# Operands of the output weights made straight from float64 in the expert layer, converted in the tile of their results; token sums moved

## The chip, the cores and the metric

One of the 8 cores of a Trainium2 chip runs the whole program. The metric is the device time of one execution in microseconds (us), as the median of several executions. One execution was also taken by the hardware profiler; it gives the rows below.

## The reference

Three stages follow each other on 2304 tokens of width 512.

```python
# 1: attention inside chunks of 64 tokens, 4 x 8 heads of width 64
scores = scale * np.matmul(q_c, k_c.transpose(0, 1, 2, 4, 3))
attn = np.exp(scores - np.max(scores, axis=-1, keepdims=True))
attn = attn / (np.sum(attn, axis=-1, keepdims=True) + 1e-09)
x = heads_joined(np.matmul(attn, v_c))              # (2304, 512)
# 2: expert layer, 4 experts, hidden width 1024
p = domain_probs / (domain_probs.sum(-1, keepdims=True) + 1e-09)
for e in range(4):
    out += p[:, e:e + 1] * (np.maximum(x @ w1[e], 0.0) @ w2[e])
# 3: gated layer, hidden width 1536, on the result of 2
g = x @ w_gate
y = (g * (1.0 / (1.0 + np.exp(-g))) * (x @ w_val)) @ w_out
```

`w_gate`, `w_val` and `w_out` come as float64 (two words a number), all else as float32.

## The kernel before

**Numbers.** TensorE multiplies in the form float32r. So that nothing is lost, each operand is split into a high part `h`, rounded by ScalarE, and a low part `l`, the rest, subtracted by GpSimd or VectorE (`split`, `w_split`, lines 126 and 127). Each product takes three matmuls: h h, h l, l h.

**Products.** Layers 2 and 3 use Strassen's scheme on 2 x 2 blocks, with 7 products (`PRODUCTS`) in place of 8. Its operands are blocks and sums of blocks: of the weights (`w_sums`, `w_split`) and of the tokens (`b11` to `b22`, `t1` to `t4`). A *set* is the 7 products of 256 hidden columns. The tokens go through in 3 passes of 768. The expert layer has 16 sets a pass (numbers 0 to 47), the gated layer 12 (48 to 83: a set of `w_gate` and one of `w_val` in turn). A product is 6 matmuls of 384 columns into a bank x, z or w (`half_k`, lines 632 to 634). Between products stand the matmuls of the second half of the layer, a *group* (two sets, or four in the gated layer's count) later: `layer2` (512 columns, lines 681 to 685) for the experts, `layer_out` (256 columns, line 747) for `w_out`.

**Order.** The program writes out the order by hand (`order`). `now` counts products. At each product, work planned with `later(d, ...)` for this count is issued, then the weights of the product six further on are loaded (`LEAD`, `prepare`, `load_w`, line 413), then background tasks take steps (`run_tasks`). All these transfers go through the one queue of SyncE (SP), which issues them in the order of the program and stands wherever one has to wait for its buffer or its data. Weight tiles `w` have 12 buffers, tiles of tokens on their way (`xt`) three, tiles for raw weights (`raw1`) two.

**Background tasks.** A task is a generator. `WAIT` lets a product pass, `STEP` asks for one of the steps that a product grants; four tasks may run. They are:
- `x_sums(p)` (line 181 on): loads blocks of pass p's tokens into two `xt` tiles, makes the four sums `t1` to `t4` on GpSimd, stores them. Twice per pass, for two halves.
- `convert`: makes float32 from float64 by bit operations: a raw load of 512 KB into a `raw64` tile, then 4 instructions on VectorE, 3 on ScalarE, 2 on GpSimd (lines 440 to 454), into `dst`.
- `make_set64(q, m)`: two conversions into a `raw1` tile, the sums, 7 splits, 7 stores into `w_d`, for a set of the gated layer.
- `make_wo(c)`: one conversion of a row block of `w_out`, stored as float32 in `wo_d`.
- `make_wo_ops(g, k)`: loads two such blocks back, makes `t1` to `t4` and splits 7 operands (low parts in turn on GpSimd and VectorE), stores them in `wo_ops`, from which `fetch_wo` loads them for each group.

`make_wo` runs in the expert layer, `make_wo_ops` from set 48 on. At the turn from one pass to the next, `x_fetch` loads the 7 operands of the new pass's tokens into `xt` tiles (line 209) and `x_split` splits them, each after the last use of the old one.

**Start.** Attention of the first six blocks of 128 tokens runs alone, with k and v of blocks 2 and 3 in tiles of their own (`att_load`, `att_load_v`), then twelve products without Strassen (`next_plain`).

## Time and profile before

| | |
|---|---|
| median of 3 executions | 1288.68 us (1286.35 to 1290.72) |
| the profiled execution | 1290.5 us, of which the span from first to last instruction is 1288.7 us |
| mean granted clock of TensorE | 0.985 |
| TensorE busy, matmuls / weight loads | 1242.0 us (96%) / 1142.7 us (89%) |
| VectorE, ScalarE, GpSimd busy | 801.1 us (62%), 538.2 us (42%), 583.5 us (45%) |
| moved by DMA | 366.24 MB, 284 GB/s in the mean |

PE is TensorE's matmuls, PEld its weight loads, DVE VectorE, ACT ScalarE, POOL GpSimd, SP the engine that issues nearly all transfers (SPq is its queue). Matmuls overlap, so a busy PE alone does not tell its speed; that is why windows of equal work are compared. A wait is told with what ended it. Names such as `w<-w` are output and input of an instruction by the program's names, buffer numbers left out.

### The profile page before, as it was taken

The numbers are of one execution on the slowest core, as the hardware profiler recorded it, in microseconds if no ns is written. First come the engines' busy times: TensorE is split into PE (matmuls) and PEld (weight loads), VectorE is DVE, ScalarE is ACT, GpSimd is POOL, SyncE is SP. The second block draws the span as 40 slices with busy tenths as digits, with TensorE's granted clock in tenths as the row PEclk, the third lists the DMA queues.
The fourth block names the chain that finished last, engine by engine and source line by source line (L and its number), as shares of the span: only waits on it lengthen the run. The fifth ranks groups of instructions, "written<-read, shape, count | busy, mean of one in ns | idle before, by whom it ended". The sixth has DMA issues, their size and how long they took to land.

```text
span 1288.7 us, 21183 instructions
## 1 busy us (share of the span) xinstructions
PE 1242.0 (96%) x7216; PEld 1142.7 (89%) x7216; DVE 801.1 (62%) x1370; ACT 538.2 (42%) x1192; POOL 583.5 (45%) x593
## 2 busy tenths in 40 slices
PE   7999999998999999999999999999885899999998
PEld 6888888897998999998999888998785899999998
DVE  5775666656655666764665654576573755676566
ACT  4554443445433444443443443455332344344331
POOL 5454343567633555552554654435652522332121
PEclk9999999999999999999999999999896999999999
DMA  8588877789898798888999788788995997698774
GB/s 230 167 280 278 269 261 244 235 296 359 302 320 302 277 335 306 306 296 272 320 318 350 276 303 291 253 288 301 365 344 177 320 347 270 241 318 289 260 248 154
DMA packets 183051, 366.24 MB, mean 284 GB/s; under 512 B 19600, under 2 KB 46736, under 8 KB 182944
## 3 DMA queue, kind: packets, MB, share of 16 engines
q1 hardware_dynamic: 182144, 363.54, 81.1%
q10 hardware_dynamic: 768, 1.31, 0.4%
q8 instruction: 58, 0.95, 0.3%
q14 instruction: 49, 0.40, 0.1%
q0 software_dynamic: 32, 0.04, 0.0%
HBM read 262.05 MB, written 102.76 MB: 283 GB/s over the span
## 4 chain that ended last, share of the span: by engine, by line
PE 81%; DMA 9%; DVE 3%; issue 2%; POOL 2%; SPq 1%; ACT 1%; POOLq 0%; DVEq 0%; ACTq 0%
PE y L681 10%; PE y L685 10%; PE y L683 10%; PE lx L632 7%; PE lx L634 7%; PE lx L633 7%; PE ox L747 4%; PE lz L632 4%; PE lz L634 4%; PE lz L633 4%; PE oz L747 3%; DMA w<-w 3%; PE lw L632 2%; PE lw L634 2%; PE lw L633 2%
## 5 line engine op out<-in xcount | busy, mean ns | idle before, releaser
L681 PE MATMUL y<-w,hh 128*128 128x512 f32 x576 | 228.7, 397 | 2.1 <-ACT hh L567 2.1
L683 PE MATMUL y<-w,hh 128*128 128x512 f32 x576 | 226.3, 393 | 1.7 <-POOL w L127 1.7
L685 PE MATMUL y<-w,hl 128*128 128x512 f32 x576 | 227.1, 394 | 0.0
L127 POOL TENSOR_TENSOR w<-raw,w 128x256 fp32r<-128x256 f32 (+1 forms) x156 | 142.9, 931 | 146.8 <-ACT w L126 121.0
L127 POOL TENSOR_TENSOR ol<-sg,oh 128x384 fp32r<-128x384 f32 x72 | 82.5, 1154 | 230.7 <-ACT oh L126 201.9
L567 ACT ACTIVATE hh<-sum_p 128x384 fp32r<-128x384 f32 x90 | 47.3, 525 | 233.4 <-DVE sum_p L620 233.2
L770 DVE SCALAR_TENSOR_TENSOR acc<-y,prob,acc 128x512 f32<-128x512 f32 x126 | 91.2, 743 | 68.4 <-PE y L685 67.9
L685 PEld LDWEIGHTS y<-w,hl 128*128 128x128 f32 x576 | 108.4, 188 | 24.2
L681 PEld LDWEIGHTS y<-w,hh 128*128 128x128 f32 x576 | 108.5, 188 | 24.0 <-ACT hh L567 2.5
L683 PEld LDWEIGHTS y<-w,hh 128*128 128x128 f32 x576 | 108.5, 188 | 22.8 <-POOL w L127 2.0
L127 POOL TENSOR_TENSOR w_made<-raw,w_made 128x256 fp32r<-128x256 f32 x84 | 67.5, 814 | 103.5 <-ACT w_made L126 94.1
L620 DVE TENSOR_TENSOR sum_p<-lx,p 128x384 f32<-128x384 f32 x81 | 44.9, 555 | 106.3 <-PE lx L634 106.1
L568 DVE SCALAR_TENSOR_TENSOR hl<-sum_p,hh 128x384 fp32r<-128x384 f32 x90 | 58.8, 654 | 61.4 <-ACT hh L567 61.4
L126 ACT ACTIVATE w<-raw 128x256 fp32r<-128x256 f32 (+1 forms) x156 | 67.4, 453 | 3.8 <-POOL w L127 2.5
L453 POOL TENSOR_TENSOR neg<-neg,raw 128x512 f32<-128x512 f32 x24 | 32.3, 1345 | 75.3 <-ACT p L616 32.9
L632 PE MATMUL lz<-t1h,w 128*128 128x384 f32 x162 | 56.3, 348 | 8.3 <-DMA w<-w 8.3
L126 ACT ACTIVATE oh<-sg 128x384 fp32r<-128x384 f32 x72 | 36.5, 524 | 63.6 <-DVE sg L581 63.3
L632 PE MATMUL lx<-t3h,w 128*128 128x384 f32 x162 | 55.5, 342 | 7.8 <-DMA w<-w 7.4
L616 ACT COPY u<-lx 128x384 f32<-128x384 f32 x81 | 38.4, 474 | 58.1 <-PE lx L634 58.1
L632 PE MATMUL lx<-t2h,w 128*128 128x384 f32 x162 | 56.3, 347 | 4.6 <-DMA w<-w 3.3
L632 PE MATMUL lx<-t4h,w 128*128 128x384 f32 x162 | 54.9, 339 | 3.7 <-DMA w<-w 3.7
L632 PE MATMUL lz<-b22h,w 128*128 128x384 f32 x162 | 56.2, 347 | 1.8 <-ACT p L616 1.6
(271 smaller groups left out, 3436.0 us busy)
## 6 DMA issues: line engine op xcount, KB each, us to landing
w<-w SPq DMA_DIRECT2D x567, 256.0 KB, 5.2
w<-w SPq DMA_DIRECT2D x96, 512.0 KB, 5.7
w<-w_made SPq DMA_DIRECT2D x84, 256.0 KB, 5.4
wo_t<-wo_t SPq DMA_DIRECT2D x36, 512.0 KB, 5.2
wo_b<-wo_b SPq DMA_DIRECT2D x27, 512.0 KB, 4.1
raw<-w SPq DMA_DIRECT2D x19, 512.0 KB, 4.3
raw<-w SPq DMA_DIRECT2D x32, 256.0 KB, 4.2
sums<-x SPq DMA_DIRECT2D x40, 192.0 KB, 5.7
```

The lines of the kernel that those rows point to most:

```text
L126: nc.scalar.activation(h, src, AF.Copy)
L127: (lo or nc.vector).tensor_tensor(out=l, in0=src, in1=h.bitcast(F32), op=ALU.subtract)
L567: nc.scalar.activation(h, src, AF.Relu)
L568: nc.vector.scalar_tensor_tensor(out=l, in0=src, scalar=0.0, in1=h.bitcast(F32), op0=ALU.max, op1=ALU.subtract)
L632: nc.tensor.matmul(ps, w[:, 0, c], xh[:, k], start=f, stop=False, skip_group_check=True)
L633: nc.tensor.matmul(ps, w[:, 0, c], xl[:, k], start=False, stop=False, skip_group_check=True)
L634: nc.tensor.matmul(ps, w[:, 1, c], xh[:, k], start=False, stop=e, skip_group_check=True)
L681: nc.tensor.matmul(y, hh[:, c], w[:, 0], start=(j == 0), stop=False)
L683: nc.tensor.matmul(y, hh[:, c], w[:, 1], start=False, stop=False)
L685: nc.tensor.matmul(y, hl[:, c], w[:, 0], start=False, stop=(j == 3))
L747: nc.tensor.matmul(o, left[:, c], w[:, k, right], start=start and t % 2 == 0 and k == 0 and i == 0, stop=k == 1 and i == 2, skip_group_che ...
L770: nc.vector.scalar_tensor_tensor(out=sum_, in0=y, scalar=p, in1=sum_, op0=ALU.mult, op1=ALU.add)
```

## The change

- `make_wo` and `wo_d` are gone. `make_set64` and `make_wo_ops` are now one function, `make_ops`: it loads both raw halves (two times 512 KB) at once into the tile that will hold the results, converts them there, makes the sums, splits 7 operands with all low parts on GpSimd, and stores them. So the operands of `w_out` come from float64 in one go.
- All 18 such tasks run in the expert layer, from set 18 on, a task of `w_out` between the two of a pair of sets. Three may be under way: every third takes the `raw64` tile (one buffer), the others `raw1`. A new kind of step, `SPLIT`, is granted once per product at most. Steps are 2 per product throughout.
- The token sums of pass 2 start with these tasks (two sets later than before), those of pass 4 follow those of pass 3 in the expert layer, those of pass 5 start alone at set 53.
- At the start, v of blocks 2 and 3 comes in two transfers in place of four, `fetch_w1(0)` stands ahead of the first scores, and the first two splits of its weights move ahead by a block.

```diff
@@ -119,7 +119,6 @@
     w2_d = [dram.tile([P, 2, DM], F32, name=f"w2_{c}") for c in range(4 * NG1)]
-    wo_d = [dram.tile([P, DM], F32, name=f"wo_{c}") for c in range(F2 // P)]
     wo_ops = [{b: dram.tile([P, 2, 2, DM // 2], F32, name=f"wo_{b}_{g}") for b in OUT_OPS} for g in range(NG2)]
@@ -196,7 +195,7 @@
                 sub(b[o], b[x], b[y], nc.gpsimd)
-            for _ in range(1 if p > NPASS else 3):
+            for _ in range(3):
                 yield WAIT
@@ -248,6 +247,15 @@
         att[a]["v"] = v
+    def load_values_23():
+        for h in range(2):
+            b = slice(64 * h, 64 * h + 64)
+            nc.sync.dma_start(
+                v23[b, :, h].rearrange("p a i c t -> p a (i c t)"), vt[2:4, b].rearrange("a p i c t -> p a (i c t)")
+            )
+        for i in range(2):
+            att[2 + i]["v"] = vbd[2 + i]
@@ -417,26 +425,22 @@
-    WAIT, STEP = range(2)
-    RAWS, LANDING = 2, 3
-    loads, sets64 = [0], [0]
-    def freed():
-        loads[0] -= 1
-    def convert(dst, src, name):
-        while loads[0] == RAWS:
+    WAIT, STEP, SPLIT = range(3)
+    LANDING = 4
+    sets64, count64, converts = [0], [0], [0]
+    def converted():
+        converts[0] -= 1
+    def convert(raw, dst, name):
+        while converts[0] == 2:
             yield WAIT
-        loads[0] += 1
-        raw = raw64_p.tile([P, 512, 2], U32, tag="raw64", name=f"raw_{name}", bufs=RAWS)
-        nc.sync.dma_start(raw.rearrange("p f w -> p (f w)"), src.bitcast(U32))
-        for _ in range(LANDING):
-            yield WAIT
-        yield STEP
+        converts[0] += 1
         low, up = raw[:, :, 0], raw[:, :, 1].bitcast(F32)
...
         topb, negb = top.bitcast(I32), neg.bitcast(I32)
+        yield STEP
         nc.vector.tensor_scalar(out=top, in0=up, scalar1=F64_MAX, scalar2=-F64_MAX, op0=ALU.min, op1=ALU.max)
@@ -451,52 +455,49 @@
         nc.gpsimd.tensor_tensor(out=neg, in0=neg, in1=low.bitcast(F32), op=ALU.mult)
-        nc.gpsimd.tensor_tensor(out=top if dst is None else dst, in0=top, in1=neg, op=ALU.add)
-        later(2, freed)
-        return top
-    def make_set64(q, m):
-        while sets64[0] == 2:
+        nc.gpsimd.tensor_tensor(out=dst, in0=top, in1=neg, op=ALU.add)
+        later(1, converted)
+    def make_ops(sources, name, sums, stores):
+        while sets64[0] == 3:
             yield WAIT
         sets64[0] += 1
-        r = raw1_p.tile([P, 8, 2 * P], F32, tag="raw1", name=f"raw_{q}_{m}")
+        count64[0] += 1
+        pool, tag = (raw64_p, dict(tag="raw64", bufs=1)) if count64[0] % 3 == 0 else (raw1_p, dict(tag="raw1"))
+        r = pool.tile([P, 8, 2 * P], F32, name=f"raw_{name}", **tag)
+        raws = [r[:, 4 * half : 4 * half + 4].bitcast(U32).rearrange("p b f -> p (b f)") for half in range(2)]
+        for half in range(2):
+            nc.sync.dma_start(raws[half], sources[half].bitcast(U32))
+        for _ in range(LANDING):
+            yield WAIT
         for half in range(2):
             dst = r[:, 2 * half : 2 * half + 2].rearrange("p b f -> p (b f)")
-            yield from convert(dst, (wg, wv)[m][q, half], f"{q}_{m}_{half}")
+            yield from convert(raws[half].rearrange("p (f w) -> p f w", w=2), dst, f"{name}_{half}")
         for half in range(2):
             yield STEP
-            w_sums(r, nc.gpsimd, half)
-        for i in range(NPROD):
-            yield STEP
-            t = w_split(r, PRODUCTS[i][1], f"made_{q}_{m}")
-            later(3, lambda i=i, t=t: nc.sync.dma_start(w_d[NPAIRS + 2 * q + m][i], t.bitcast(F32)))
+            sums(r, half)
+        for a, to in stores:
+            yield SPLIT
+            t = w_split(r, a, f"made_{name}")
+            later(3, lambda to=to, t=t: nc.sync.dma_start(to, t.bitcast(F32)))
         sets64[0] -= 1
-    def make_wo(c):
-        t = yield from convert(None, wo[c], f"wo_{c}")
-        yield WAIT
-        yield WAIT
-        nc.sync.dma_start(wo_d[c], t)
+    def make_set64(q, m):
+        into = w_d[NPAIRS + 2 * q + m]
+        stores = [(PRODUCTS[i][1], into[i]) for i in range(NPROD)]
+        return make_ops((wg, wv)[m][q], f"{q}_{m}", lambda r, half: w_sums(r, nc.gpsimd, half), stores)
     def make_wo_ops(g, k):
-        while sets64[0] == 2:
-            yield WAIT
-        sets64[0] += 1
-        r = raw1_p.tile([P, 8, 2 * P], F32, tag="raw1", name=f"raw_wo_{g}_{k}")
-        for c in range(2):
-            nc.sync.dma_start(r[:, 2 * c : 2 * c + 2].rearrange("p b f -> p (b f)"), wo_d[4 * g + 2 * k + c])
-        for _ in range(LANDING + 1):
-            yield WAIT
         places = {"b11": 0, "b12": 1, "b21": 2, "b22": 3, "t1": 4, "t2": 5, "t3": 6, "t4": 7}
-        for o, x, y in ("t1", "b12", "b11"), ("t2", "b22", "t1"), ("t3", "b22", "b12"), ("t4", "b21", "t2"):
-            yield STEP
-            sub(r[:, places[o]], r[:, places[x]], r[:, places[y]], nc.gpsimd)
-        for i, b in enumerate(OUT_OPS):
-            yield STEP
-            t = w_split(r, places[b], f"wo_{g}_{k}", nc.vector if i % 2 else nc.gpsimd)
-            later(5, lambda b=b, t=t: nc.sync.dma_start(wo_ops[g][b][:, k], t.bitcast(F32)))
-        sets64[0] -= 1
+        ops = ("t1", "b12", "b11"), ("t2", "b22", "t1"), ("t3", "b22", "b12"), ("t4", "b21", "t2")
+        def sums(r, half):
+            for names in ops[2 * half : 2 * half + 2]:
+                o, x, y = (r[:, places[b]] for b in names)
+                sub(o, x, y, nc.gpsimd)
+        c = 4 * g + 2 * k
+        return make_ops(wo[c : c + 2], f"wo_{g}_{k}", sums, [(places[b], wo_ops[g][b][:, k]) for b in OUT_OPS])
@@ -806,9 +807,10 @@
             vbd.append(at_p.tile([P, 2, NPAIR, 2, D], F32, tag=f"v{i}", name=f"vbd{i}", bufs=1))
+        v23 = first_p.tile([P, 2, 2, NPAIR, 2, D], F32, name="v23", bufs=1)
         for i in range(2):
             kbd.append(first_p.tile([P, 2, NPAIR, 2, CH], F32, name=f"kbd{2 + i}", bufs=1))
-            vbd.append(first_p.tile([P, 2, NPAIR, 2, D], F32, name=f"vbd{2 + i}", bufs=1))
+            vbd.append(v23[:, i])
@@ -834,7 +836,8 @@
         att_load(3)
-        att_load_v(2)
+        load_values_23()
+        fetch_w1(0)
@@ -875,8 +878,6 @@
         att_scores(0, where())
-        fetch_w1(0)
-        att_load_v(3)
         att_soft(0)
@@ -889,6 +890,8 @@
                 fetch_w1(1)
+            elif i == 2:
+                w_plain(0, ORDER[:2])
         att_values(2, where())
@@ -896,7 +899,6 @@
         att_exp(4)
-        w_plain(0, ORDER[:2])
         att_scores(5, where())
@@ -966,23 +968,21 @@
-        EARLY = 4
         make64 = []
         for q in range(NPAIRS2):
-            for m in range(2):
-                make64.append(make_set64(q, m))
-                if EARLY <= 2 * q + m + EARLY < 2 * NPAIRS2:
-                    make64.append(make_wo(2 * q + m + EARLY))
+            make64 += [make_set64(q, 0), make_wo_ops(q // 2, q % 2), make_set64(q, 1)]
...
                 running.append([tasks.pop(0), WAIT])
+            splits = 1
             for r in list(running):
-                if r[1] == STEP:
-                    if steps == 0:
+                if r[1] != WAIT:
+                    if steps == 0 or r[1] == SPLIT and splits == 0:
                         continue
                     steps -= 1
+                    splits -= r[1] == SPLIT
                 r[1] = next(r[0], None)
@@ -1071,7 +1071,6 @@
                 wow_p = ctx.enter_context(tc.tile_pool(name="wow", bufs=2, side="right"))
-                tasks += [make_wo_ops(g, k) for g in range(NG2) for k in range(2)]
             product(n, i)
@@ -1106,19 +1105,17 @@
                     tasks.append(x_sums(1))
-            if o == (NPAIRS, 1):
-                tasks += [x_sums(2)] + [make_wo(c) for c in range(EARLY)]
-            elif o == (NPAIRS + 2, 1):
-                tasks += make64
+            if o == (NPAIRS + 2, 1):
+                tasks += [x_sums(2)] + make64
             elif o == (2 * NPAIRS + 3, 1):
-                tasks.insert(0, x_sums(3))
-            elif o == (N1 + 3, 6):
-                tasks.insert(0, (y for p in (4, 5) for y in x_sums(p)))
+                tasks.insert(0, (y for p in (3, 4) for y in x_sums(p)))
+            elif o == (N1 + 5, 4):
+                tasks.append(x_sums(5))
             elif o == (N1 + 3, 2):
...
             if not (last_of_pass(n) or last_of_pass(n + 1) and i >= 5 or now[0] - turned[0] < 2):
-                run_tasks(2 if n < N1 + 4 else 1 + now[0] % 2)
+                run_tasks(2)
             now[0] += 1
```

How SP's queue changes, at three places (`x_70` and `x_69` are token stores of passes 5 and 4, `w_79`, `w_80`, `w_97`, `w_104` the made weights of sets 18, 19, 52, 59, `w_93` those of sets 48, 60 and 72). At the turn from pass 3 to pass 4, before:

```order
L202 DMA xt_75<-sums_4_1_10628 128x384
L192 DMA sums_5_0_10789<-x_70 128x384 x2
L192 DMA sums_5_0_10792<-x_70 128x384 x2
L413 DMA w_2_10805<-w_104 128x512
L512 DMA wo_t_10807<-wo_t_1_162 128x1024
L413 DMA w_3_10842<-w_104 128x512
L209 DMA xraw_b_4_10853<-x_69 128x768
L209 DMA xraw_b_4_10855<-x_69 128x768
L209 DMA xraw_t_4_10857<-xt_75 128x768
L413 DMA w_4_10860<-w_104 128x512
```

and now:

```order
L513 DMA wo_b_10687<-wo_b_1_149 128x1024
L421 DMA w_1_10721<-w_104 128x512
L421 DMA w_6_10740<-w_103 128x512
L421 DMA w_2_10752<-w_104 128x512
L513 DMA wo_t_10754<-wo_t_1_150 128x1024
L421 DMA w_3_10789<-w_104 128x512
L208 DMA xraw_b_4_10800<-x_69 128x768
L208 DMA xraw_b_4_10802<-x_69 128x768
L208 DMA xraw_t_4_10804<-xt_75 128x768
L421 DMA w_4_10807<-w_104 128x512
```

The loads of the sums of pass 5 no longer stand ahead of the fetches of pass 4; before, these sums were stored some 30 rows further down, behind all fetches. Now they are loaded and stored some 20 to 55 rows above the fetches; the last of them:

```order
L513 DMA wo_t_10471<-wo_t_1_146 128x1024
L421 DMA w_3_10506<-w_102 128x512
L421 DMA w_4_10518<-w_102 128x512
L201 DMA xt_76<-sums_5_1_10335 128x384
L201 DMA xt_76<-sums_5_1_10338 128x384
L201 DMA xt_76<-sums_5_1_10335 128x384
L201 DMA xt_76<-sums_5_1_10338 128x384
L421 DMA w_5_10535<-w_102 128x512
```

The last row here follows the last store of the sums; nothing of them is under way at the turn. In the gated layer's first pass (weights of set 52), before:

```order
L413 DMA w_0_9599<-w_97 128x512
L488 DMA raw_wo_0_9607<-wo_141 128x512
L488 DMA raw_wo_0_9607<-wo_142 128x512
L488 DMA raw_wo_1_9610<-wo_143 128x512
L488 DMA raw_wo_1_9610<-wo_144 128x512
L413 DMA w_1_9635<-w_97 128x512
L413 DMA w_6_9646<-w_96 128x512
L512 DMA wo_b_9648<-wo_b_0_149 128x1024
L512 DMA wo_t_9650<-wo_t_0_150 128x1024
L498 DMA wo_b_0_153<-w_wo_0_3_9561 128x512
L498 DMA wo_b_0_153<-w_wo_1_3_9564 128x512
L413 DMA w_2_9664<-w_97 128x512
```

and now:

```order
L421 DMA w_0_9704<-w_97 128x512
L421 DMA w_1_9728<-w_97 128x512
L421 DMA w_6_9739<-w_96 128x512
L513 DMA wo_b_9741<-wo_b_0_137 128x1024
L513 DMA wo_t_9743<-wo_t_0_138 128x1024
L421 DMA w_2_9755<-w_97 128x512
```

The loads and stores that make operands of `w_out` are gone from between the weight loads. In the expert layer, at set 18, before:

```order
L413 DMA w_1_4158<-w_80 128x512
L407 DMA w_79<-w_7_4093 128x512
L432 DMA raw_wo_4175<-wo 128x1024
L520 DMA w_9_1_4186<-w_5_110 128x1024
L413 DMA w_2_4194<-w_80 128x512
```

and now:

```order
L421 DMA w_1_4115<-w_80 128x512
L415 DMA w_79<-w_7_4055 128x512
L191 DMA sums_2_0_4129<-x_67 128x384 x2
L191 DMA sums_2_0_4132<-x_67 128x384 x2
L470 DMA raw_0_4135<-wg 128x1024 x2
L470 DMA raw_wo_0_4138<-wo 128x1024 x2
L470 DMA raw_1_4141<-wv 128x1024 x2
L521 DMA w_9_1_4153<-w_5_110 128x1024
L421 DMA w_2_4161<-w_80 128x512
```

Six raw loads and four loads of tokens now stand in one piece between two weight loads. The order of the matmuls is the same in both kernels.

## Rows read from the trace of the kernel before

**Rows 1.** The page, 40 slices of the span: busy tenths of TensorE's matmuls.
```profile
PE   7999999998999999999999999999885899999998
```
**Rows 2.** Windows (us): length, PE, PEld, DVE, ACT, POOL busy (instructions), clock, DMA share, GB/s.
```profile
864.40:1045.20 180.80, 151.35 (x900) 144.16 (x900) 107.76 (x188) 66.40 (x151) 83.72 (x81) 0.92 0.86 308
1045.20:1179.80 134.60, 133.09 (x883) 131.96 (x883) 89.63 (x176) 56.19 (x121) 39.23 (x33) 1.00 0.79 279
350.20:562.30 212.10, 212.10 (x1067) 191.42 (x1065) 130.79 (x210) 89.91 (x188) 98.38 (x94) 1.00 0.87 306
562.30:797.00 234.70, 234.70 (x1183) 211.52 (x1183) 136.39 (x213) 99.58 (x216) 124.04 (x125) 1.00 0.87 302
676.60:708.80 32.20, 32.20 (x162) 29.00 (x161) 17.56 (x29) 11.90 (x27) 14.34 (x16) 1.00 0.99 350
902.10:934.30 32.20, 26.89 (x150) 25.44 (x150) 18.50 (x32) 12.42 (x32) 20.55 (x22) 0.89 1.00 365
...
966.50:998.70 32.20, 17.50 (x67) 16.44 (x66) 10.00 (x17) 6.54 (x11) 7.61 (x6) 0.69 0.53 178
```
**Rows 3.** Waits of PE, 860 to 1035 us: total us, times, longest us.
```profile
PE lx L632 <- DMA w<-w: 14.5, 4, 7.4
PE lz L632 <- DMA w<-w: 8.3, 6, 3.3
```
**Rows 4.** Timeline of PE: start, duration (us), line, operation, tiles.
```profile
958.52 0.33 PE L632 MATMUL lx<-t3h,w 128*128 128x384 f32 x1
...
985.12 0.52 PE L632 MATMUL lx<-t3h,w 128*128 128x384 f32 x1
```
**Rows 5.** Timeline of SP's queue at the turn from pass 3 to pass 4.
```profile
964.14 0.80 SPq L192 DMA_DIRECT2D sums<-x  x2
...
966.41 8.06 SPq L209 DMA_DIRECT2D xraw_b<-x  x2
980.24 0.32 SPq L209 DMA_DIRECT2D xraw_t<-xt  x1
```
**Rows 6.** Chain of work that ended last, 860 to 1040 us: start, us, what.
```profile
966.41 5.86 DMA xraw_b<-x
```
**Rows 7.** Waits of PE, 1045 to 1180 us.
```profile
PE lz L632 <- DMA w<-w: 0.2, 1, 0.2
```
**Rows 8.** DMA issues: count, KB each, median us from issue to landing.
```profile
w<-w SPq DMA_DIRECT2D x567, 256.0 KB, 5.2
...
sums<-x SPq DMA_DIRECT2D x40, 192.0 KB, 5.7
...
wo_t<-w_wo SPq DMA_DIRECT2D x24, 256.0 KB, 5.2
...
wo_b<-w_wo SPq DMA_DIRECT2D x18, 256.0 KB, 5.8
...
wo<-top_wo SPq DMA_DIRECT2D x12, 256.0 KB, 3.8
raw_wo<-wo SPq DMA_DIRECT2D x12, 256.0 KB, 4.7
```
**Rows 9.** Waits of SP's queue, 350 to 797 us.
```profile
SPq L472 <- POOL w_made L127: 63.2, 36, 6.6
...
SPq L432 <- POOL neg L453: 34.8, 14, 6.0
```
**Rows 10.** Groups on POOL, 350 to 797 us: count, busy us, mean ns, idle before.
```profile
L127 POOL TENSOR_TENSOR w_made<-raw,w_made 128x256 fp32r<-128x256 f32 x83 | 66.7, 814 | 98.7 <-ACT w_made L126 89.3 <-DMA w<-w_made 5.0 <-DMA w<-w 4.3
L397 POOL TENSOR_TENSOR raw<-raw 128x256 f32<-128x256 f32 x48 | 37.8, 809 | 1.8
```
**Rows 11.** One group on DVE, 864 to 1031 us, then 1040 to 1120 us.
```profile
L130 DVE TENSOR_TENSOR sg<-sg,sg 128x384 f32<-128x384 f32 x17 | 15.0, 882 | 5.2 <-POOL ol L127 5.0
...
L130 DVE TENSOR_TENSOR sg<-sg,sg 128x384 f32<-128x384 f32 x12 | 6.7, 556 | 6.1 <-POOL ol L127 5.9
```
**Rows 12.** Timeline of PE in the first slice.
```profile
23.01 1.93 PE L262 MATMUL s<-kbd,q 128*64 128x128 f32 x16 [2.05 <-DMA kbd<-kt]
```

## Prediction before the change was run

> **What bounds the kernel now.** I read the page's slices first, then the windows. TensorE is busy in nearly every slice; the holes are the first slice, one near 300 us, and a group between 870 and 1030 us [rows 1]. The windows say what that group costs [rows 2]. From 350.2 to 797.0 us (weights of the gated layer are made beside the expert layer) PE is busy for all of 212.10 and 234.70 us, although the DMA engines are at 0.87. From 864.4 to 1045.2 us it is busy 151.35 of 180.80 us at a clock of 0.92. The next window, 1045.2 to 1179.8 us, holds the same work one pass later, 84 products and their share of the output layer (set 64 to set 76 instead of 52 to 64), and takes 134.60 us, 133.09 of them busy, at clock 1.00. The counts are close: 900 matmuls against 883, the first having the expert layer's last transposes too. So 180.80 - 134.60 = **46.2 us** are lost in the first pass of the gated layer, and the matmuls' order does not explain it. Of them 29.45 - 1.51 = 27.9 us are idle time and the other 18.3 lie in slower matmuls, 0.65 us for each us of stop.
>
> What PE waits for there: 14.5 us in 4 waits at products into bank x, the longest 7.4, and 8.3 us in 6 at bank z, all for weight loads [rows 3]. Behind the longest, at 985.12 us, a matmul takes 0.52 us that took 0.33 at 958.52 [rows 4]: after such a stop TensorE is at the lower of its two clock levels. Why the weights are late shows on the SP queue [rows 5]. At 964.14 us it issues loads of `sums`, at 966.41 it stands 8.06 us over two loads of `xraw_b`, then nothing before 980.24. The chain of waits gives the first of them 5.86 us [rows 6]; the second is issued some 8 us after the first, once that one is split. The operands of the next pass are fetched one by one because the tag `xt` has three buffers and the token sums of pass 5 hold two across the turn of the pass (first order piece). All weight loads stand behind them. One pass later no sums are under way, and the only wait of PE for a weight load from 1045 to 1180 us is 0.2 us [rows 7].
>
> The smaller part lies before that turn: while the operands of w_out are made, DMA runs full. From 902.1 to 934.3 us share 1.00, 365 GB/s, PE busy 26.89 of 32.20 us [rows 2].
>
> **The change part by part.** The sum is made against the profiled execution: 1290.5 us, of which the span is 1288.7; the median of the runs is 1288.68, so 1.8 us come off at the end.
>
> *Operands of w_out leave the second part.* Out of it go 12 loads of 256 KB (`raw_wo`), 42 stores of 256 KB [rows 8], 42 splits, 24 subtractions; SP issues 24 transfers fewer in all, since the copies in `wo_d` are neither stored nor read. The token sums of pass 4 go with them, and those of pass 5 start at set 53 and are stored before the first fetch of the turn (order pieces). What is left is the work of the twin, so I let the stretch fall to the twin's time: **-46.2 us**.
>
> *Sums of pass 5 stay inside the stretch*, the twin has none: 8 loads and 8 stores of 192 KB [rows 8], 3.1 MB, some 9 us of the queue at 350 GB/s, in a stretch whose DMA share is 0.79. Between 0 (hidden) and 9 us; I take **+1**, since 0.79 leaves room.
>
> *The first part takes over that work.* Removed there: 12 stores of 256 KB (`wo<-top_wo`). Added: 42 stores of 256 KB and the sums of pass 4, 16 transfers of 192 KB [rows 8]; the 12 conversions were there already. Net 42 x 256 - 12 x 256 + 16 x 192 KB, some 11 MB. Over 446.8 us that is 25 GB/s on 304, so share 0.87 becomes about 0.94. The window 676.6 to 708.8 us stood at 0.99 and 350 GB/s with PE busy for all 32.20 us [rows 2]: hidden there. GpSimd gets 42 splits at 814 ns and 24 subtractions at 809 ns [rows 10], 53.6 us on its 98.38 + 124.04 us: from 50% to 62%, off the path as far as no product waits for it (the rival below).
>
> Here a rule speaks against the change. The page DMA: Bandwidth & Descriptors of the Trainium skill (Specifications) gives a core some 358 GB/s of HBM bandwidth. By it, as an estimate, windows that run at 350 GB/s now and are asked for 375 would last 1.05 times as long; if a third of the first part were so, that is 7 us, and the sum below would end at 1253.5. The trace does not hold the chip to that figure, since the window at 902.1 us moved 365 GB/s.
>
> VectorE loses 18 of the 42 low parts to GpSimd, and the two slow each other: the subtraction `sg` took 882 ns from 864 to 1031 us and 556 from 1040 to 1120 [rows 11], where GpSimd is busy 46% and 29% of the stretch [rows 2]. VectorE is busy 267 of 446.8 us in the first part; made longer by 882/556 in the 12% more of the time that GpSimd is busy, 19 us more, 60 to 64%. PE waits for nothing there now, so I cost it at nothing; without that cover it is at most these 19 us.
>
> *Where a set starts.* The raw 512 KB loads now land in the tile of the results, two at once, one product after the last split that read the tile; before it was two products after a conversion. The SP queue already stood for such loads, 34.8 us in 14 times, longest 6.0, and for stores of made weights, 63.2 us in 36 [rows 9], with no wait on PE. Products take 446.8/198 = 2.26 us, weights are loaded six ahead, 13.5 us, and land after 5.2 [rows 8]: 8.3 us in hand. A mean stop of 2.5 us, one product more (2.3) and 0.5 MB more ahead (1.4) leave 2.1; the longest stop (6.0) ends 1.4 us too late. Of 18 starts, with the first three and two token tiles in one product (third order piece), I expect a few late by one or two us, some at the low clock: **+4**. The ends: 0 (the window at 0.99 without a wait) and the rate of 902.1 to 934.3 us (5.3 us idle in 32.2) over all 446.8 us, 74 us. The first is far nearer: same kinds of work, same queue.
>
> *The start.* The first weights and v of blocks 2 and 3 are fetched ahead of k of blocks 4 and 5, with two loads fewer. PE waits 2.05 us for k at 23.01 us [rows 12]; the load can be earlier by its place or later by the 512 KB ahead of it. Between -2 and +2; **-1**. The hole at 318 us has its cause in slow loads and splits at the turn of a pass, before the point where tasks now begin; it stays.
>
> Sum: 1290.5 - 46.2 + 1 + 4 - 1 = 1248.3 for the profiled kind of run, less 1.8: **1246.5 us**.
>
> **The rivals.**
> *The queue becomes the bound of the first part.* For it: 0.94 on average means stretches at 1.00, and at 902.1 us such a stretch cost PE 5.3 us in 32.2. Against: 676.6 to 708.8 us, and at most one split per product now. If a third of the 446.8 us ran at that rate, 24.5 us: 1271; a milder half of that 1259. The rule on 358 GB/s, above, would be its mildest form.
> *The turn still costs.* If the turn from pass 3 to 4 is slow for another reason (fetch and split of seven operands), what is lost from 966.5 to 998.7 us stays: 32.20 - 17.50 = 14.7 us idle and 0.31 of 17.50, 5.4, by the clock of 0.69 [rows 2], 20 us: 1266.5. Against it: the same turn from 4 to 5 runs through [rows 7].
> *Slower: SP stands at each start of a set.* If GpSimd is behind when a set starts, SP waits for its last split, and every weight load behind it is late. It decides once the 2.1 us in hand above are gone at nearly every start, that is with GpSimd about a product further behind. Price: 2.5 us of stop and 0.65 of that for the clock, 4.1 us, 18 times, 74 us: 1242.5 + 74 = 1316. Against it: 50 stops of SP (98.0 us) and no wait on PE today [rows 9].
>
> **How the numbers follow.** Forecast 0.71 (alone 1238 to 1256: the start at its ends, 0 to 12 us given back), full queue 0.18, turn 0.07, slower 0.04. The range 1237 to 1266 leaves out the slower case, part of the turn's and the worse third of the full queue's at the top, and little below. Faster by over 0.3% (4 us, about what a measurement of this kernel can tell from no change): 0.95; within: 0.01; slower: 0.04.
>
> **What would show it.** Right: the window from set 52 to set 64 takes 135 to 138 us at clock 1.00; the waits of PE for weight loads (22.8 us in rows 3) fall under 3 us; SP never stands 8 us at `xraw_b` of pass 4; the window of the first part shows DMA about 0.94, GpSimd about 62%, PE busy nearly throughout. Wrong: PE waits for `w` in the first part adding up to over 10 us, low-clock stretches there, or a stop of several us at the turn with no `sums` under way.

## The result and the profile after

The changed kernel takes **1250.21 us** (median of 6 executions, 1247.11 to 1252.53); the kernel before, run beside it, 1291.2 us (6 executions, 1286.35 to 1294.83). The ratio is **0.9685**, 95% interval 0.966 to 0.971. The predicted 1246.5 us is 3.7 us lower, and the range held the result. The profiled execution took 1251.89 us, of which the span is 1250.1.

The page of the profile after, its 40 slices (TensorE's matmuls, its granted clock, the DMA engines), to be held against [rows 1]:

```profile
PE   8999999999899999999999999999999999999998
...
PEclk9999999999899999999999999999999999999999
DMA  8488786788797999897899999866888797788774
```

The holes of [rows 1] past 860 us are gone; what is left is the first slice, the last, and one hole near 318 us.

The windows between the same products as in [rows 2] (length, then busy time of PE, PEld, DVE, ACT, POOL, clock, DMA share, GB/s): set 52 to 64, its twin 64 to 76, and set 18 to 48, where the weights of the gated layer and the operands of w_out are made.

```profile
868.10:1006.30 138.20, 136.29 (x900) 134.31 (x899) 95.90 (x176) 57.15 (x123) 47.90 (x41) 1.00 0.84 295
1006.30:1141.00 134.70, 132.89 (x885) 131.96 (x884) 89.76 (x176) 56.19 (x121) 39.15 (x33) 1.00 0.81 277
...
349.90:818.40 468.50, 466.43 (x2338) 418.98 (x2337) 290.44 (x441) 210.81 (x460) 292.94 (x301) 1.00 0.92 330
```

The stretch from set 52 fell from 180.80 us to 138.20 at clock 1.00, **-42.6 us**. The stretch from set 18 to 48 grew from 464.5 us (350.2 to 814.7 in the trace before) to 468.5, **+4.0**. Set 3 begins at 68.4 us instead of 69.9, **-1.5**. From there to set 18 it is 1.2 us longer (281.5 against 280.3), all at the hole near 318 us, and 0.3 us lie elsewhere. The 1.2 us are within the scatter: the 17 products around the hole (from set 16, experiment 8) take 47.9 us here and 45.6 to 47.7 in the ten other traces that have it, 46.7 in that of the kernel before. The sum is -38.6, the difference of the two spans (1250.1 - 1288.7).

What PE waits for in the stretch from set 52, against 22.8 us in [rows 3]:

```profile
PE ox L748 <- DVE acc L722: 0.8, 2, 0.5
PE lz L633 <- ACT p L617: 0.8, 1, 0.8
PE lz L633 <- DMA w<-w: 0.4, 1, 0.4
```

And the SP queue at that turn, where [rows 5] had a stop of 8.06 us and then nothing for 5.8 us; then its longest wait from 930 to 975 us (L208 is the fetch):

```profile
941.89 0.90 SPq L208 DMA_DIRECT2D xraw_b<-x  x2
942.84 0.43 SPq L208 DMA_DIRECT2D xraw_t<-xt  x1
...
952.59 0.32 SPq L208 DMA_DIRECT2D xraw_t<-xt  x1
...
955.60 0.32 SPq L208 DMA_DIRECT2D xraw_t<-xt  x1
```
```profile
SPq L208 <- DVE b11l L126: 5.9, 1, 5.9
```

The first three operands now go out in one piece, one into each `xt` tile; before, the second had to wait for the first. At the fourth SP still stands 5.9 us, until the split of `b11` has freed a tile, and the last ones follow 2.8 to 3 us apart. Loads of weights (left out here) go before and between them, and PE waits only 0.4 us for a weight in the whole stretch.

In the stretch from set 18 to 48 (asked from 350 to 800 us for SP), the waits of the SP queue now, against [rows 9]:

```profile
SPq L470 <- POOL w_made L126: 33.7, 9, 5.8
...
SPq L470 <- POOL w_made_wo L126: 12.4, 5, 4.8
```

L470 is the raw load that lands in the tile of the results. It stood 14 times for 46.1 us, the longest 5.8 (before, 14 times for 34.8).

### The profile page after: what moved, and what is told of

Read it like the earlier page. It is cut to its first block, busy times and chain, and to the rows that moved or that the text cites. A ratio compares the mean times of both kernels' runs of the same rounds, so it can differ in the third digit from the quotient of the medians.

```text
span 1250.1 us, 21098 instructions
## 1 busy us (share of the span) xinstructions
PE 1229.3 (98%) x7216; PEld 1133.4 (91%) x7216; DVE 791.4 (63%) x1352; ACT 538.4 (43%) x1192; POOL 594.5 (48%) x611
## 4 chain that ended last, share of the span: by engine, by line
PE 86%; DMA 5%; DVE 3%; issue 2%; POOL 1%; ACT 1%; SPq 1%; POOLq 0%; DVEq 0%; ACTq 0%
PE y L682 9%; PE y L686 9%; PE y L684 9%; PE lx L633 8%; PE lx L635 8%; PE lx L634 8%; PE ox L748 5%; PE oz L748 4%; PE lz L633 4%; PE lz L635 4%; PE lz L634 4%; PE lw L633 2%; PE lw L635 2%; PE lw L634 2%; DMA xraw_b<-x 1%
## 5 line engine op out<-in xcount | busy, mean ns | idle before, releaser
L684 PEld LDWEIGHTS y<-w,hh 128*128 128x128 f32 x576 | 108.7, 189 | 22.6 <-POOL w L126 1.9
L569 DVE SCALAR_TENSOR_TENSOR hl<-sum_p,hh 128x384 fp32r<-128x384 f32 x90 | 62.1, 690 | 65.8 <-ACT hh L568 65.8
L125 ACT ACTIVATE oh<-sg 128x384 fp32r<-128x384 f32 x72 | 36.5, 525 | 70.4 <-DVE sg L582 70.1
L633 PE MATMUL lw<-b21h,w 128*128 128x384 f32 x162 | 54.9, 339 | 1.2 <-DMA w<-w 1.1
L125 ACT ACTIVATE o<-sg 128x384 fp32r<-128x384 f32 x54 | 26.5, 520 | 66.9 <-DVE sg L129 66.8
```

The source lines that it names most:

```text
L125: nc.scalar.activation(h, src, AF.Copy)
L569: nc.vector.scalar_tensor_tensor(out=l, in0=src, scalar=0.0, in1=h.bitcast(F32), op0=ALU.max, op1=ALU.subtract)
L633: nc.tensor.matmul(ps, w[:, 0, c], xh[:, k], start=f, stop=False, skip_group_check=True)
L684: nc.tensor.matmul(y, hh[:, c], w[:, 1], start=False, stop=False)
```

## The experiments

Each ran beside the kernel before on the same chip, on four chips in all; times are medians. The kernel before took 1290.3 to 1292.5 us in these series, so differences of 2 us or less between series say little by themselves.

**1. The collision at the turn, put back alone.** The token sums of pass 5 start five sets later, so that they hold two `xt` tiles across the turn, as before; the work for w_out stays in the first part.

```diff
-            elif o == (N1 + 5, 4):
+            elif o == (N1 + 10, 4):
                 tasks.append(x_sums(5))
```

> The changed kernel, but the token sums of pass 5 begin at product 4 of set 58 instead of set 53, so that two of the three xt tiles are held across the turn from pass 3 to pass 4; nothing is made for w_out in this stretch. Theory (the held tiles make the fetches of the new operands go one by one, and the weight loads stand behind them): the turn loses the 20 us that it lost before (14.7 idle and 5.4 by the clock), 1250 + 20 = about 1270, with PE waits for w of some 15 us between 930 and 1000 us and SP standing several us at the fetches of xraw. Rival (the turn was slow only because the queue was full with operands of w_out): about 1250 to 1252.

Measured: 1264.59 us (1263.81 to 1268.35), ratio 0.9812 (0.9789 to 0.9835): 14.4 us over the change. The window from set 52 to 64, the longest of PE's waits in it, and the SP queue:

```profile
864.90:1018.70 153.80, 142.04 (x902) 140.31 (x901) 92.13 (x176) 57.10 (x123) 47.57 (x41) 0.94 0.76 261
```
```profile
PE lx L633 <- DMA w<-w: 8.6, 2, 4.7
```
```profile
940.04 9.07 SPq L208 DMA_DIRECT2D xraw_b<-x  x2
...
954.79 0.32 SPq L208 DMA_DIRECT2D xraw_t<-xt  x1
...
959.84 0.32 SPq L208 DMA_DIRECT2D xraw_t<-xt  x1
```

The operands are again fetched one by one (9.07 us over the first two, then 5 to 6 us apart), the weights behind them are late (11.7 us of waits in all), and the clock is at the lower level in part of the stretch (0.94 in the mean). 15.6 of the 42.6 us come back (153.8 - 138.2), less than the 20 expected.

**2. The turn cleared alone, in the kernel before.** The work for w_out stays in the gated layer; the token sums of pass 4 and 5 are parted, and those of pass 5 wait until the turn is over.

```diff
             elif o == (N1 + 3, 6):
-                tasks.insert(0, (y for p in (4, 5) for y in x_sums(p)))
+                tasks.insert(0, x_sums(4))
+            elif o == (N1 + 13, 0):
+                tasks.append(x_sums(5))
```

> The kernel before, but the token sums of pass 5 begin after the turn (product 0 of set 61); the operands of w_out are still made in the gated layer. Theory: 20 of the 46 us are won, about 1271, the waits of PE between 890 and 960 us stay (some 10 us idle). Rival (the load on the queue makes the turn slow): the turn still loses, 1285 to 1291.

Measured: 1272.45 us (1268.73 to 1275.16), ratio 0.9865 (0.984 to 0.9891). The window from set 52 to 64:

```profile
864.20:1025.70 161.50, 144.43 (x901) 137.96 (x900) 109.16 (x188) 66.35 (x151) 83.40 (x81) 0.97 0.95 339
```

180.8 - 161.5 = 19.3 us for the turn; and from experiment 1, 180.8 - 153.8 = 27.0 us for the work that moved away (that for w_out, and the token sums of pass 4). 19.3 + 27.0 = 46.3 against 42.6 with both: the two overlap by 3.7 us. So the turn is worth 15.6 to 19.3 us and the work 23.3 to 27.0, by whether the other is still there. What of the work costs is not parted: in experiment 2 PE waits 11.5 us for weights and 5.4 for VectorE and ScalarE.

**3. More bytes in the first part.** Each of the 42 operands of w_out is stored a second time, to a place that nothing reads: 11 MB, 42 issues more, and tiles held longer.

```diff
...
             later(3, lambda to=to, t=t: nc.sync.dma_start(to, t.bitcast(F32)))
+            if name[:2] == "wo":
+                later(3, lambda to=twice.pop(), t=t: nc.sync.dma_start(to, t.bitcast(F32)))
```

> The changed kernel, but each of the 42 made operands of w_out is stored a second time, into memory that nothing reads: 42 stores of 256 KB more, 11 MB, in the 468 us of the expert layer from set 18 on (0.92 of the DMA engines now, 0.98 then). Theory (the queue still has room on average, what is lost there is lost at single late loads): 2 to 8 us more, 1252 to 1258. Rival (the queue is already the bound of the first part): the bytes cost their full time, 11 MB at 350 GB/s, 31 us, about 1281.

Measured: 1264.02 us (1261.84 to 1264.99), ratio 0.98 (0.978 to 0.9819), 13.8 us over the change. Window from set 18 to 48, and what PE waits for in it:

```profile
347.30:831.20 483.90, 470.79 (x2338) 421.34 (x2338) 291.18 (x441) 211.46 (x460) 292.35 (x301) 0.99 0.94 342
```
```profile
PE lx L636 <- DMA w<-w: 7.2, 6, 2.4
PE lw L636 <- DMA w<-w: 5.2, 2, 4.4
PE lz L636 <- DMA w<-w: 0.6, 1, 0.6
```

The result lies between the two theories: 15.4 us in this stretch, 13.0 of them waits for weights. 11 MB at 350 GB/s are 31 us, so half of the added transfers was hidden and half was not. The change leaves the queue room for only part of them. As the extra stores also hold their tiles longer, the run does not tell bytes from tiles.

**4. A later start of sets.** A set counts as done two products after its last split, so that SP meets the raw loads of the next one later.

```diff
...
-        sets64[0] -= 1
+        later(2, set_done)
```

> The changed kernel, but a set counts as done two products after its last split, so that the raw loads of the next one are issued three products behind the last reader of their tile instead of one. Theory (the 4 us lost in the first part come from SP standing at those raw loads, 46.1 us in 14 times): SP stands there under 20 us, the first part (set 18 to set 48) takes 464 to 466 us instead of 468.5, the kernel 1246 to 1249. Rival (what is lost there comes from the bytes): no change, 1250, within 1 us.

Measured: 1250.21 us (1249.22 to 1251.1), ratio 0.9696 (0.9674 to 0.9717): no difference. The stops at the raw loads are no longer among the longest waits of the SP queue; SP stands for the stores of made weights (L485) instead:

```profile
SPq L485 <- POOL w_made L126: 52.4, 30, 8.6
```

The stretch from set 18 to 48 takes 467.5 us, one less, within what traces of the change's own program show (467.3 to 468.5, see experiment 7). So the stops at set starts do not by themselves explain the 4.0 us. Alone, that is: see experiments 11 and 12.

**5. Without the limit on splits.** The change grants one split per product at most; here any of the two steps may be one.

```diff
-            splits = 1
+            splits = 9
```

> The change's new limit of one SPLIT per product is taken away; the two steps per product stay. Theory (the 4.0 us that the first part, set 18 to set 48, grew by, come from the bytes on a queue that is nearly full): the bytes are the same, so the part stays within 2 us of 468.5 and the time within 2 us of 1250.2. Rival (the limit keeps the made weights from holding several w tiles at once, and the loads from standing behind their stores): without it weights are late, PE waits for w by 5 us or more between sets 18 and 48, and the time is 1255 to 1270.

Measured: 1259.58 us (1257.39 to 1261.68), ratio 0.9768 (0.974 to 0.9796): 9.4 us slower than the change, which is what the rival said. From set 18 to 48:

```profile
347.80:824.00 476.20, 468.64 (x2338) 418.28 (x2337) 291.42 (x441) 209.29 (x460) 295.25 (x301) 1.00 0.91 324
```
```profile
PE lx L633 <- DMA w<-w: 2.9, 4, 1.4
PE lw L633 <- DMA w<-w: 1.9, 2, 1.3
...
PE lz L633 <- DMA w<-w: 1.1, 2, 0.6
```

The bytes are the same and the DMA share is 0.91, but 5.9 us of waits for weights appear (1.1 in the change). Which it is, tiles held or stores in front of the loads, this run does not part.

**6. Token sums of pass 5 out of the stretch**, to set 61, behind the turn.

```diff
-            elif o == (N1 + 5, 4):
+            elif o == (N1 + 13, 0):
```

> Pass 5's token sums are moved from set 53 to set 61, behind the turn of the pass. Theory (what the stretch from set 52 to set 64 has over its twin, 138.2 against 134.7 us, is the 16 extra transposes and a few short waits at the turn, and the sums cost nothing): the stretch stays at 137 to 139 us and the time within 1.5 us of 1250.2. Rival (the sums' 3.1 MB and their two xt tiles cost the stretch the 2 or 3 us): 135 to 136 us in the stretch and a time of 1247 to 1248.

Measured: 1250.7 us (1248.36 to 1252.74), ratio 0.9693 (0.9668 to 0.9719): no difference. The stretch from set 52 to 64:

```profile
868.30:1005.80 137.50, 135.71 (x901) 134.32 (x900) 91.80 (x176) 57.20 (x123) 47.05 (x41) 1.00 0.84 291
```

That is 0.7 us less, and more than scatter: in the seven other traces with these sums at set 53 the stretch takes 138.1 or 138.2 us, and in experiments 11 and 12, which also have them behind the turn, 137.4. What it still has over its twin shows in the trace of the change (PE from 868 to 874 us):

```profile
869.11 0.60 PE L296 MATMUL x1t<-ident,acc 128*128 128x128 f32 x4
869.46 0.42 PE L633 MATMUL lw<-b21h,w 128*128 128x384 f32 x1
...
870.59 0.39 PE L682 MATMUL y<-w,hh 128*128 128x512 f32 x1
```

The expert layer ends inside this stretch: 8 transposes (4 in 0.35 us, 0.7 us) and 9 matmuls of 512 columns, 0.23 us apart (2.1 us), 2.8 us in all. They are the 17 matmuls by which the counts of [rows 2] differ (900 and 883; the expectation took them for 16 transposes). With the 0.7 us of the sums that makes the 3.5 us between 138.2 and 134.7.

**7. Fewer bytes in the first part.** Only the first group's operands of w_out are stored, and every group loads and multiplies with those; 35 stores and 9.2 MB less, the engines' work the same.

```diff
-            later(3, lambda to=to, t=t: nc.sync.dma_start(to, t.bitcast(F32)))
+            if to is not None:
+                later(3, lambda to=to, t=t: nc.sync.dma_start(to, t.bitcast(F32)))
...
-        return make_ops(wo[c : c + 2], f"wo_{g}_{k}", sums, [(places[b], wo_ops[g][b][:, k]) for b in OUT_OPS])
+        return make_ops(wo[c : c + 2], f"wo_{g}_{k}", sums, [(places[b], wo_ops[0][b][:, k] if g == 0 else None) for b in OUT_OPS])
...
-        nc.sync.dma_start(t.bitcast(F32), wo_ops[part_of(G)[2]][b])
+        nc.sync.dma_start(t.bitcast(F32), wo_ops[0][b])
```

> Only the first group's 7 operands of w_out are stored and every later group loads those, so 35 of the 42 stores of 256 KB (9.2 MB) leave the first part; the conversions, sums and splits stay (the output layer multiplies with the first group's operands throughout). Theory (the first part grew by 4.0 us through bytes: 11 MB more on a queue that the run with twice the stores showed to be near its end): from set 18 to set 48 it takes 465 to 466 us, and the time is 1246 to 1248. Rival (the growth comes from the tasks' instructions, GpSimd at 62% and splits that share engines with the products, and the bytes were hidden): the part stays at 468 to 469 and the time at 1250.

Measured: 1250.19 us (1248.61 to 1250.69), ratio 0.9688 (0.9665 to 0.9711): no difference in the time. In the trace the stretch from set 18 to 48 takes 466.7 us, 1.8 less. To see which part that is, I cut it into pieces, first in the trace of the change (sets 18 to 24, to 38, to 43):

```profile
349.90:446.90 97.00, 96.32 (x484) 86.27 (x483) 58.88 (x91) 41.74 (x91) 53.66 (x55) 1.00 0.91 329
446.90:675.00 228.10, 228.06 (x1148) 204.99 (x1147) 144.58 (x219) 106.82 (x233) 148.89 (x152) 1.00 0.90 326
675.00:754.90 79.90, 78.54 (x392) 70.34 (x391) 50.86 (x78) 35.62 (x77) 58.83 (x62) 1.00 0.99 361
```

The first and third pieces of the kernel before:

```profile
350.20:445.70 95.50, 95.50 (x484) 86.33 (x483) 54.79 (x92) 39.20 (x80) 35.45 (x32) 1.00 0.86 298
...
673.20:751.20 78.00, 78.00 (x391) 70.38 (x391) 43.72 (x70) 31.72 (x71) 44.67 (x48) 1.00 0.90 314
```

And the third piece with fewer bytes:

```profile
674.40:752.40 78.00, 78.00 (x391) 70.38 (x391) 50.98 (x78) 35.45 (x77) 58.80 (x62) 1.00 0.96 347
```

The 4.0 us are 1.5 in the first piece and 1.9 in the third (the second 0.6). Four more traces have the same program here (experiments 1, 6, 8 and 9): their first piece takes 97.0 to 97.8 us, their third 79.1 to 79.9, the whole stretch 467.3 to 468.2. So the growth is 2.8 to 4.0 us, and the 78.0 of this run lies outside the scatter. The third piece loses its time with 0.99 of the DMA engines' time used and is well again with 0.96, though GpSimd has the same 58.8 us of work. Whether the bytes did it, or the tiles and places in the queue that the 35 stores took, this run does not part; a share of 0.99 over 32 us cost nothing in the kernel before [rows 2]. The first piece (97.4 us in this run) is not cured.

**8. The hole near 318 us.** It is there before and after. In the trace of the change: PE's waits from 300 to 350 us, SP's queue, the fetch of `b22` in the chain of waits, ScalarE.

```profile
PE y L682 <- ACT hh L568: 3.0, 1, 3.0
PE y L684 <- POOL w L126: 1.4, 1, 1.4
```
```profile
286.75 5.15 SPq L201 DMA_DIRECT2D xt<-sums  x4
```
```profile
306.29 7.67 DMA xraw_b<-x
```
```profile
313.98 0.84 ACT L125 ACTIVATE b22h<-xraw_b 128x768 fp32r<-128x768 f32 x1 [4.68 <-DMA xraw_b<-x]
```

The four stores of pass 1's sums hold SP for 5.15 us as the turn's fetches begin; the fetch of `b22` is issued only at 306.29, ScalarE stands for it with the `hh` behind it that PE needs. The edit starts the second half of these sums four products earlier:

```diff
-            for _ in range(4 * k):
+            for _ in range(4 * k if p > 1 else 0):
                 yield WAIT
```

> The token sums of pass 1 start 4 products earlier in their second half, so that SP is not held by their four stores (5.15 us at 286.75) while operands of the turn to pass 1 are fetched. Theory (the hole of PE at 316.8 to 320.5 us, 4.4 us idle and a low clock up to 323.6, comes from the load of b22 being late behind those stores): the hole closes and the time is 1243 to 1247. Rival (the load is slow by itself, 7.7 us among other loads, and ScalarE stands for it with hh behind it wherever the stores are): hole unchanged, 1249 to 1251.

Measured: **1245.35 us** (1244.54 to 1246.58), ratio 0.9653 (0.9631 to 0.9676). ScalarE's wait for `b22`, and the window of 17 products from set 16, of this run; then that window in the change:

```profile
308.29 0.85 ACT L125 ACTIVATE b22h<-xraw_b 128x768 fp32r<-128x768 f32 x1 [1.35 <-DMA xraw_b<-x]
```
```profile
301.90:342.60 40.70, 40.50 (x209) 36.13 (x208) 24.50 (x37) 19.33 (x45) 24.61 (x23) 1.00 0.81 285
```
```profile
302.00:349.90 47.90, 43.46 (x210) 37.97 (x210) 25.66 (x40) 19.71 (x45) 26.46 (x26) 0.93 0.79 280
```

The hole closes: 7.2 us in the profiled executions, 4.9 in the medians. The fetch of `b22` is issued at 301.99 us here, 4.3 earlier.

**9. The old start.** All edits of the start undone.

```diff
...
-        load_values_23()
-        fetch_w1(0)
+        att_load_v(2)
...
         att_scores(0, where())
+        fetch_w1(0)
+        att_load_v(3)
...
-            elif i == 2:
-                w_plain(0, ORDER[:2])
...
         att_exp(4)
+        w_plain(0, ORDER[:2])
```

> The edits of the start are undone (v of blocks 2 and 3 in four loads, the first weights behind the first scores, the two splits a block later), all else is the change. Theory (the start gave 1 us): the first product of set 3 begins at 69 to 70 us, where the runs with the new start so far had it at 67.1 to 70.4 (mean 68.2), and the time is 1251 to 1252. Rival (the start moved nothing; the 1.5 us between the two profiles is scatter of the first 70 us from one execution to the next): anywhere in 67 to 70 us, and a time within 1 us of 1250.2.

Measured: 1252.21 us (1250.69 to 1253.79), ratio 0.9696 (0.9675 to 0.9716). Set 3 begins at 70.8 us. The window 24.6 to 28.0 us of this run, then of the change:

```profile
24.60:28.00 3.40, 3.05 (x9) 2.74 (x10) 1.58 (x4) 1.85 (x5) 2.81 (x4) 0.50 1.00 242
```
```profile
24.60:28.00 3.40, 3.40 (x32) 2.98 (x31) 2.65 (x6) 2.02 (x6) 1.41 (x2) 1.00 0.94 244
```

The three traces with the old start have set 3 at 68.9, 69.9 and 70.8 us, the last two with the lower clock near this place; the eleven with the new start at 67.1 to 70.4, mean 68.2, one (70.4) with the lower clock. That is 1.7 us in the mean, the way of the theory, but it does not settle it: part of it goes with the clock (70.4 against 69.9 and 70.8 with a stretch at the lower level, 67.1 to 68.9 against 68.9 without), three traces cannot tell whether the edit made that stretch rarer, and the medians, 2.0 us apart, have overlapping ranges.

**10. The first three sets started apart**, 5 products each.

```diff
-                tasks += [x_sums(2)] + make64
+                tasks += [x_sums(2)] + make64[:1]
+            elif o == (NPAIRS + 2, 6):
+                tasks.append(make64[1])
+            elif o == (NPAIRS + 3, 4):
+                tasks += make64[2:]
```

> The first three sets of made operands, which the change starts within one product (six loads of 512 KB and two of token blocks within some 5 us, during which the queue ran at 379 to 408 GB/s), are started 5 products apart. Theory (this burst makes the weight late for which PE waits 0.5 us at 367.03, and about half of the 4 us by which the first part grew): no wait of PE between sets 18 and 24, that piece (97.0 us) takes 95.5 to 96, and the time is 1248.5 to 1249.5. Rival (the half microsecond belongs to the bytes as a whole and only moves): 97 us and 1250.

Measured: 1250.52 us (1249.8 to 1252.92), ratio 0.9687 (0.9667 to 0.9708). The first and third pieces:

```profile
348.20:443.70 95.50, 95.50 (x484) 86.34 (x484) 60.54 (x91) 41.13 (x90) 53.77 (x54) 1.00 0.93 330
671.60:752.60 81.00, 78.64 (x393) 70.38 (x392) 52.02 (x78) 35.94 (x78) 59.01 (x62) 1.00 0.99 353
```

The first piece is as before the change (95.50; 96.7 to 97.8 in the eight traces with all three sets started at once and no added stores), so the burst of raw loads was its cause. But the third took 1.1 us more than in the change, and the time did not move: most of the predicted gain was given back there.

**11. All together**: experiments 8 and 10 (their edits left out here), the token sums of pass 4 moved from the first part to set 51, those of pass 5 to set 61.

```diff
-                tasks.insert(0, (y for p in (3, 4) for y in x_sums(p)))
-            elif o == (N1 + 5, 4):
+                tasks.insert(0, x_sums(3))
+            elif o == (N1 + 3, 6):
+                tasks.append(x_sums(4))
+            elif o == (N1 + 13, 0):
                 tasks.append(x_sums(5))
```

> All that helped, together: the token sums of pass 1 four products earlier (1245.35 alone), the first three sets apart, the token sums of pass 4 moved out of the full first part to set 51 and those of pass 5 to set 61. Theory (the costs lie in different places and add up: 1.3 us at the starts, 1.4 at the wait for a weight near 725 us where the queue runs at 361 GB/s, 0.7 in the stretch): 1241 to 1244, with no wait of PE for a weight between sets 18 and 48. Rival (what the first part gives back, the stretch from set 52 takes with the sums of pass 4): 1244.5 to 1246.

Measured: 1245.63 us (1243.98 to 1246.48), ratio 0.9645 (0.9625 to 0.9665), no better than experiment 8 alone. That is the rival's number but not its reason: the stretch from set 52, with the sums of pass 4 in it, takes 137.4 us. One place has what the others gave: PE waits 1.9 us for a weight at 716.54 us. SP's longest stop before it, and the windows around it:

```profile
SPq L470 <- POOL w_made_wo L126: 6.2, 1, 6.2
```
```profile
704.00:710.00 6.00, 6.00 (x32) 5.49 (x31) 5.30 (x8) 4.05 (x9) 5.84 (x7) 1.00 0.21 61
710.00:716.00 6.00, 4.68 (x24) 3.87 (x22) 3.94 (x6) 1.01 (x3) 5.92 (x7) 1.00 0.99 334
716.00:722.00 6.00, 5.46 (x20) 4.96 (x21) 4.61 (x8) 4.18 (x10) 3.06 (x4) 0.72 1.05 409
```

While SP stands at the raw loads, the DMA engines run dry (61 GB/s) although the weights behind could be fetched; then they are full, PE waits, and its clock falls (0.72 in the last window). That is no want of bandwidth but the stop at the start of a set.

**12. The same with the later start of sets** (the edit of experiment 4).

> The run with all that helped (1245.63 us), and with it the later start of sets (two products after a set's last split, which alone changed nothing). In that run SP stood 6.2 us from 701 to 708 us at the raw loads of a set whose tile GpSimd had not finished; the DMA engines moved 61 GB/s in the 6 us from 704 to 710, the weight loads stood behind, and PE waited 1.86 us for a weight at 716.54, with a low clock to 720.7. Theory (this stop is the late-start case of the prediction, at one place): no stop of SP at raw loads over 3 us, no wait of PE for a weight there, the piece from 665 to 748 us (83.0) takes 78 to 79.5, and the time is 1241.5 to 1243.5. Rival (the stop only moves to the stores of made weights, and the weight is late all the same): 81 to 83 us in that piece and 1244.5 to 1246.5.

Measured: **1241.07 us** (1240.69 to 1243.15), ratio **0.9612** (0.9593 to 0.9632). The window at the same place, the piece from set 38 to 43, and all that PE waits for from 335 to 800 us:

```profile
704.00:710.00 6.00, 6.00 (x33) 5.44 (x32) 5.30 (x8) 3.94 (x10) 5.84 (x7) 1.00 0.93 330
...
665.40:744.80 79.40, 78.35 (x393) 70.42 (x392) 58.69 (x82) 38.50 (x85) 60.50 (x63) 1.00 0.97 347
```
```profile
PE lz L636 <- ACT p L620: 1.0, 1, 1.0
```

The piece takes 79.4 us (83.0 without the edit), the stretch from set 18 to 48 takes 465.9, and no wait for a weight is left in it. The edit that did nothing alone is worth 4.6 us here.

## Why the prediction was right, and where it was off

**Bound.** Right as to the two causes: the turn with its operands fetched one by one, 15.6 to 19.3 us, and the work for w_out with the token sums of pass 4, 23.3 to 27.0 us (experiments 1 and 2). Their order was wrong: the prediction calls the part before the turn the smaller, and it is the larger. As the change removes both, the sum did not suffer. One sign named for being wrong, a stop of several us at the turn with no sums under way, did show on the SP queue (5.9 us), yet it cost no time: three fetches and loads of weights had gone ahead of it, and PE waited 0.4 us for a weight.

**Operands of w_out leave.** This is the mis-sized term. "What is left is the work of the twin, so I let the stretch fall to the twin's time" counted as a loss what was work: the 8 transposes and 9 matmuls by which 900 and 883 differ are 2.8 us. The prediction named the transposes and gave them no price. 46.2 - 2.8 - 0.7 for the sums = 42.7, against the measured 42.6.

**Sums of pass 5.** +1 forecast, 0.7 measured (experiment 6).

**First part.** +4 forecast, 4.0 measured. That it agrees to a tenth is luck: the ends given were 0 and 74 us, and five traces of the same program give 2.8 to 4.0 (experiment 7). The DMA share came out at 0.92 (forecast 0.94). GpSimd was busier than forecast: in the forecast's own window, now 349.9 to 800.7 us, 291.08 of 450.8 us or 64.6%, against 62%; the working left out the token sums, of which 12 more, of 1.0 us each, run in it now. The cause forecast, a few set starts late by one or two us, is one of two. The first piece is the start of three sets within a product (experiment 10). The third lost its 1.9 us where the DMA engines ran at 0.99, and 35 stores less cure it (experiment 7); but where the sums of pass 4 had been moved away, the stop of SP at a raw load showed in their place (experiments 11 and 12). VectorE's slowing by GpSimd, costed at nothing, cost nothing that shows: busy 290.44 of 468.5 us, 62%, and PE waited 0.2 us for it.

**The full queue**, the rival with most chance, was not the case but near: with 11 MB more, half of their time comes out (experiment 3). The rule named with it is some 358 GB/s for a core (Trainium skill, DMA: Bandwidth & Descriptors, Specifications). It did not show as a limit here: 6 us windows ran at up to 409 GB/s, in the run of experiment 11, and one slice of 31 us of the change at 384. The mean rate of the stretch was 342 GB/s even in experiment 3; what cost, where a trace was read closely (experiment 11), was a short stretch in which loads came behind other transfers.

**The turn still costs**: no; it runs through. **SP stands at each start**: SP did stand 14 times at raw loads, 3.3 us in the mean, but weights had enough in hand nearly everywhere. At one place, in experiment 11, it was decisive, at 4.6 us, close to the 4.1 of the rival's price.

**The start.** -1 forecast, -1.5 in the profile, 1.7 in the mean of the traces. k was not earlier (PE goes on at 23.03 us, before at 23.01); between the two profiles what went was the stretch at the lower clock behind it (23.1 to 26.5 us before). Since that stretch comes and goes with either start (experiment 9), it is not shown that the edit removed it, and that the forecast fits is in part luck.

**The hole at 318 us.** It stayed. The prediction named slow loads and splits at the turn; experiment 8 shows what made the load late, the four stores of pass 1's sums ahead of it. It was 1.2 us longer in the profiled execution, within its scatter. With the 2.6 us by which the first two terms were off and 0.3 us elsewhere that is the miss, less half a us that the start gave more. The kernel before also took some 2 us more in these runs than in the three on which the forecast was built.

## What to carry to other kernels

To price a bad stretch by its undisturbed twin, subtract first the work that only the bad one has: matmul counts that differ by 17 in 900 were 2.8 us. On one queue in program order, ask two things apart: how full the engines are, and what stands at the head; 6 us of the DMA engines at 61 GB/s just before PE waited for a load were the mark of the second here. An edit that moves nothing alone can be worth several microseconds once the limit beside it is gone, so try such edits again together.

## What was not expected of the hardware

Equal programs in the first 30 us came out at either clock level: with the new start one trace in eleven had a stretch of 3.4 us at the lower one there, with the old one two in three. A wait near that point does not fix it: with the old start, PE waited 1.84 us for k at 22.6 us in experiment 2 and the clock stayed up, 2.05 us at 23.0 in the kernel before and it fell. So 1.5 us between two single profiles of the start mean little. And this one core's DMA engines moved 390 to 409 GB/s in single windows of 6 us (408 from 356 to 362 us in the change, at the burst of raw loads), well above the 350 GB/s on which the forecast was worked out.
